# Newton's steps for the inverse roots of the norms, and the order of the first and last pair, in an attention and feed-forward kernel

## The chip, the cores and the metric

The kernel runs on one core of one Trainium2 chip. The core has five engines with a queue each: PE (TensorE, matrix products), DVE (VectorE), ACT (ScalarE), POOL (GpSimd) and SP (SyncE, which here issues transfers). Each engine works through its queue in order, and engines wait for each other through semaphores. The metric is the device time of one execution in microseconds.

## The reference

Eight batches of twelve heads, 448 positions, 64 values a head. Queries and keys are normalised by their root mean square and scaled with gains, then comes a softmax attention. Its output, seen as 3584 tokens of 768 values, goes through a feed-forward layer with a squared ReLU.

```python
def rmsnorm(x, g):
    rms = np.sqrt(np.mean(x * x, axis=-1, keepdims=True) + 1e-06)
    return x / rms * g
q_n, k_n = (rmsnorm(q, g_q), rmsnorm(k, g_k))
scores = scale * np.matmul(q_n, k_n.transpose(0, 1, 3, 2))
attn = np.exp(scores - max) / sum
x = (attn @ v).transpose(0, 2, 1, 3).reshape(B * S, H * D)
g = np.maximum(x @ w_in, 0.0) ** 2
out = g @ w_out
```

`w_in` and `w_out` come as 64-bit floats and are turned into 32-bit floats in the kernel.

## The kernel before, in words

The work is done by pairs of heads, so that 2 x 64 = 128 rows fill the array. There are 48 pairs. The feed-forward layer is a Strassen-Winograd product over two batches at a time (a span): seven products of half-size blocks in place of eight. Its weights' sums and differences are made once and kept in memory outside the core (`w1s`, `w2s`), from where blocks are streamed (`sw`).

The order of every instruction is written out by hand: inside the schedule the engines' queues hold the instructions in program order. Python generators interleave the strands of work.

**First stage.** `attention_alone` works on the first NAT = 12 pairs (two batches) with no product beside them. For pair i it does:

- `norm(i + 2)`: squares on ACT, sums over 64 values on DVE, the mean and 1e-6 on DVE, the inverse root on POOL as a power of -0.5 (L702, one value for each row, head and query or key: 112 x 16), and the queries times their factors on POOL (L704). The keys stay raw; their factors go into the exponentials as scales.
- `transpose(i + 1, s, n)`: four PE transposes into a bank of PSUM, and a copy to `qkT` on ACT. s = 1 are the keys, which wait only for their load; s = 0 the queries, which wait for L704.
- `scores(i, c)` for four chunks c of 112 keys: two matmuls (PE) and two exponentials (ACT).
- `values(i, ...)`: exponentials times values, on PE.
- `add_up(i, c)`: DVE adds the chunks' exponentials together in `acc` (L769). `total_of(i)` multiplies by ones on PE and so sums over keys: once for `acc`, which holds chunks 0 to 2, once for chunk 3.
- `finish(i)`: DVE turns the sums, takes their reciprocals and multiplies the outputs by them. `combine_x(i)` makes the differences that the first product needs (DVE, L849 to L854).

Pairs overlap: while pair i's scores are made, pair i-1's second half of values and its totals are. The function yields four times a pair. At each yield the caller takes a few steps of `weights`: the generator `prepare` makes one 128-row slice of the weights in four steps, with ACT (L580, L596), DVE (L593, L598, L603) and POOL. On POOL it adds halves (L568) and makes sums and differences (L574); each of these instructions has 128 x 384 elements. 52 such steps (EARLY) belong in the first stage, four of them before the first pair's scores and four more with its first yield. The other 88 lie beside the first product.

The norms of pairs 0 and 1 are made by another function, `normalise_in_turn` (L335), with powers of 112 x 8; pair 0's stands ahead of all else, in `first_pair`.

**Later stages.** `first_product` (L989) and `second_product` (L1036) alternate, with the attention of the next span woven into the second product. There the norms are `norm_by_squares`: DVE sums, a power on POOL of 128 x 28 (L724) and two products (L726).

The order in POOL's queue in the first stage is, pair by pair: L702, L704, then the weights' L568 and L574 of the four yields. So a late weights instruction makes the next pair's norm late, and PE's transposes of the queries with it.

Of the kernel before, what the change touches and what calls it, by code (L numbers as in the profile page):

```python
# [9 lines left out]
F32 = mybir.dt.float32  # L10
U32 = mybir.dt.uint32
AF = mybir.ActivationFunctionType
ALU = mybir.AluOpType
AX = mybir.AxisListType.X
# [372 lines left out]
def attention_then_ffn_bounded(  # L387
# [291 lines left out]
    def load_v(i):  # L679
# [5 lines left out]
        else:  # L685
            for h in range(2):
                nc.sync.dma_start(vs[i][:, h], v[b, h0 + h].rearrange("(j p) d -> p j d", j=NJ))

    def norm(i):
        if i >= NAT:  # L690
            squares(i)
            return norm_by_squares(i)
        raw, sq = (places_of(qk, i, n)[:SP] for n in range(2))
        rstd = rstds[i] = small.tile([SP, 2, 2 * NJ], F32, tag="rstd", name="rstd", bufs=4)
        normed[i] = sq[:, 0], raw[:, 1]
        if i == 1:
            return normalise_in_turn(nc, raw, sq, rstd, mhalf)
        nc.scalar.activation(sq, raw, AF.Square)
        nc.vector.tensor_reduce(rstd, sq.rearrange("p s (n d) -> p s n d", d=D), AX, ALU.add)
        nc.vector.tensor_scalar(rstd, rstd, 1.0 / D, 1e-6, ALU.mult, ALU.add)  # L700
        flat = rstd.rearrange("p s n -> p (s n)")
        nc.gpsimd.tensor_tensor(flat, flat, mhalf[:SP, 0:4 * NJ], ALU.pow)  # L702

        nc.gpsimd.tensor_tensor(sq[:, 0].rearrange("p (j h d) -> p h j d", j=NJ, h=2),  # L704
                                raw[:, 0].rearrange("p (h j d) -> p h j d", j=NJ, h=2),
                                rstd[:, 0].rearrange("p (h j) -> p h j ()", h=2).to_broadcast([SP, 2, NJ, D]),
                                ALU.mult)
# [5 lines left out]
    def norm_by_squares(i):  # L713
        raw, qkn = (by_squares(i, n) for n in range(2))
        NG = S // 32
        half = small.tile([P, 2 * NG], F32, tag="half", name="half")
        other = small.tile([P, 2 * NG], F32, tag="other", name="other")
        nc.vector.tensor_reduce(half, qkn.rearrange("p s g e -> p (s g) e"), AX, ALU.add)
        for n in range(4):
            m = n ^ 1  # L720
            nc.vector.tensor_copy(other[n * 32:(n + 1) * 32], half[m * 32:(m + 1) * 32])
        nc.vector.tensor_tensor(half, half, other, ALU.add)
        nc.vector.tensor_scalar(half, half, 1.0 / D, 1e-6, ALU.mult, ALU.add)  # L723
        nc.gpsimd.tensor_tensor(half, half, mhalf, ALU.pow)  # L724
        for s in range(2):
            nc.gpsimd.tensor_tensor(  # L726
                qkn[:, s], raw[:, s],
                half[:, s * NG:(s + 1) * NG].rearrange("p g -> p g ()").to_broadcast([P, NG, 32]), ALU.mult)
        normed[i] = qkn

    def transposes(i):
# [16 lines left out]
    def scores(i, c):  # L748

        at = i % 2 if i < NAT else 0  # L750
        sc = ps_s.tile([SP, 2, 512], F32, tag="s", name="sc")
        for h in range(2):
            rows = slice(h * D, (h + 1) * D)
            nc.tensor.matmul(sc[:, h, 0:S], qkT[rows, at, 1, c * SP:(c + 1) * SP], qkT[rows, at, 0, :],  # L754
                             start=True, stop=True)
        pr = probs[i, c] = places[(NJ * i + c) % len(places)][:SP]
        if i < NAT:
            for h in range(2):
                nc.scalar.activation(pr[:, h], sc[:, h, 0:S], AF.Exp, scale=rstds[i][:, 1, 2 * c + h:2 * c + h + 1])  # L759
        else:  # L760
            nc.scalar.activation(pr, sc[:, :, 0:S], AF.Exp)  # L761

    def acc_of(i):
        return sums[i % 2] if i < NAT else sums["acc"]

    def add_up(i, c):

        acc = acc_of(i)[:SP]
        nc.vector.tensor_tensor(acc, probs[i, 0] if c == 1 else acc, probs[i, c], ALU.add)  # L769
# [43 lines left out]
    def total_of(i):  # L813


        tots[i] = ps_o.tile([P, S], F32, tag="t", name="tot")
        for n, pr in enumerate((acc_of(i)[:SP], probs[i, NJ - 1])):
            for h in range(2):
                nc.tensor.matmul(tots[i][h * D:(h + 1) * D, :], sums["ones"], pr[:, h, :],  # L819
                                 start=(n == 0), stop=(n == 1))  # L820

    def finish(i):

        b, hp = divmod(i, NPAIR)
        pav, factors = pavs.pop(i), xT[:, b % 2, hp]
        x = factors
        if i < NAT:


            turned, factors = sums["turned"], sums["factors"]  # L830
            few = small.tile([P, S // 32], F32, tag="few", name="few")
            nc.vector.transpose(turned, tots.pop(i))
            nc.vector.reciprocal(few, turned.rearrange("p (g r) -> p g r", r=32)[:, :, 0])
            nc.vector.transpose(factors.rearrange("p (g r) -> p g r", r=32),
                                few.rearrange("p g -> p g ()").to_broadcast([P, S // 32, 32]))

            x = x.rearrange("d (p j) -> d j p", j=NJ)
            pav, factors = (t.rearrange("d (j p) -> d j p", j=NJ) for t in (pav, factors))
        nc.vector.tensor_tensor(x, pav, factors, ALU.mult)
        del vs[i]  # L840
# [15 lines left out]
    def attention_alone():  # L856


        for i in range(NAT):
            more = i + 1 < NAT  # L860
            if i + 3 < NAT:
                load(i + 3)
            scores(i, 0)
            scores(i, 1)
            if i + 2 < NAT:
                norm(i + 2)
            elif not more:
                norm(NAT)
                load(NAT + 2)
            add_up(i, 1)  # L870
            yield
            if i:
                transpose(i + 1, 1, 0) if more else None
                values(i - 1, (2, 3))
                total_of(i - 1)
                transpose(i + 1, 0, 0) if more else None
                finish(i - 1)
            load_v(i + 1)
            yield
            scores(i, 2)  # L880
            scores(i, 3)
            if i == 0:
                transpose(1, 0, 0)
                transpose(1, 1, 1)
            values(i, (0, 1))
            yield
            add_up(i, 2)
            if i:
                combine_x(i - 1)
            if NAT <= i + 3 < NAT + 2:  # L890
                load(i + 3)
            yield
        values(i, (2, 3))
        total_of(i)
        finish(i)
        combine_x(i)
# [181 lines left out]
    with tc.tile_pool(name="words", bufs=2) as spare["pool"]:  # L1078
        for _ in range(2):
            load_w(loaded[0])  # L1080
            loaded[0] += 1
        load(2)
        norm(1)
        with tc.tile_pool(name="first", bufs=2, reuse_waits="tile") as work:

            free = [gT[:, f] for f in range(NFC) if f % HF < HF - 2]
            places[:] = [g.rearrange("p (h q) -> p h q", h=2) for g in free[:2 * NJ]]
            sums[0], sums[1] = (g.rearrange("p (h q) -> p h q", h=2) for g in free[2 * NJ:2 * NJ + 2])
            sums["turned"], sums["factors"] = (g[:, 0:S] for g in free[2 * NJ + 2:2 * NJ + 4])
            sums["ones"] = work.tile([SP, D], F32, tag="ones", name="ones", bufs=1)  # L1090
            nc.vector.memset(sums["ones"], 1.0)
            weights(4)
            for u, _ in enumerate(attention_alone()):


                weights(min(EARLY, 8 + (EARLY - 8) * (u + 1) // (4 * NAT - 4)))
                if u == 4 * NAT - 6:
                    load_blocks(5)
        with tc.tile_pool(name="first_product", bufs=2, reuse_waits="tile") as work:
            for u, _ in enumerate(first_product(work, 0)):  # L1100
                if u == 6:

                    left = ps_s.tile([P, 2, 512], F32, tag="s", name="bits")
                    banks["bits"] = left.rearrange("p a b -> p (a b)")[:, 0:NW].bitcast(U32)
                weights(min(ALL, EARLY + (ALL - EARLY) * (u - 1) // (N1 - 6)))
                if u == N1 - 5:
                    norm(NAT + 1)
                if u == N1 - 4:
                    transposes(NAT)
                    squares(NAT + 2)  # L1110
# [24 lines left out]
def kernel(  # L1135
# [27 lines left out]
    def square_of_bound():  # L1163
# [5 lines left out]
        bound.tile([128, 8, 8 * D], F32, name="qk"),  # L1169
        bound.tile([128, 2, 2, S], F32, name="qkT"),  # L1170
        bound.tile([128, 128], F32, name="ident"),
        bound.tile([128, 2 * (S // 32)], F32, name="mhalf"),
        bound.tile([128, 2], F32, name="gains"),
        bound.tile([S // 4, 2, 8], F32, name="rstd0"),
        (load_gains, square_of_bound),
# [45 lines left out]
```

## Time and profile before

| what | before |
|---|---|
| time, median of 3 | 1406.08 us (1405.57 to 1407.02) |
| profiled span | 1404.7 us |
| PE busy | 98% of the span |
| DVE, ACT, POOL busy | 58%, 30%, 42% |
| L702, power of 112 x 16 | 10 times, 3583 ns each |
| L724, power of 128 x 28 | 36 times, 4827 ns each |
| L335, power of 112 x 8 | 4 times, 1709 ns each |
| L574 and L568 on POOL, first and second weights | 64 and 64 times, 1145 and 1147 to 1288 ns each |
| first stage ends (first matmul of the first product) | 139.9 us |

The shares of busy time are means over the whole span. Which engine a stage waits for is read from that stage's own window and from the chain of waits. POOL's power takes much longer than its size suggests, as each element costs it some 0.17 to 0.2 us.

### The profile page before, as it was taken

How to read it: one execution, taken by the hardware profiler on the slowest of the kernel's cores; microseconds unless marked ns; L12 is line 12 of the kernel's file. 1: busy time of each engine (PE TensorE's matmuls, PEld its weight loads, DVE VectorE, ACT ScalarE, POOL GpSimd, SP SyncE). 2: the span in 40 equal slices, each digit the busy share in tenths (PEclk: the TensorE clock that was granted, in tenths of full speed). 3: DMA queues.
4: the chain of work that ended last, by engine and by line, in shares of the span. 5: the costliest groups of instructions: out<-in, count | busy, mean ns of one | idle time of the engine just before them, and what ended most of it. 6: DMA issues, size and time to landing. Idle time of an engine off the chain costs nothing.

```text
span 1404.7 us, 14407 instructions
## 1 busy us (share of the span) xinstructions
PE 1377.9 (98%) x4422; PEld 636.9 (45%) x4422; DVE 813.5 (58%) x1402; ACT 420.3 (30%) x620; POOL 591.0 (42%) x400
## 2 busy tenths in 40 slices
PE   7998999999999999999999999999999999999998
PEld 3333445444444455544444455444444445554554
DVE  6999677489876333576777523457777633332111
ACT  7775565433332011233332011232333201110000
POOL 7999687544453022554344112445435302221000
PEclk9999999999999999999999999999999999999999
DMA  8767899645655433345576333345565333333443
GB/s 242 215 192 199 278 378 327 184 106 119 128 115 119 102 85 90 100 109 123 108 138 121 98 94 90 98 104 112 119 128 105 96 98 90 86 90 101 106 110 72
DMA packets 430914, 188.78 MB, mean 134 GB/s; under 512 B 277484, under 2 KB 428780, under 8 KB 430828
## 3 DMA queue, kind: packets, MB, share of 16 engines
q1 hardware_dynamic: 421228, 179.05, 49.2%
q10 hardware_dynamic: 9472, 8.72, 2.4%
q8 instruction: 37, 0.61, 0.2%
q14 instruction: 49, 0.40, 0.1%
q0 software_dynamic: 128, 0.00, 0.0%
HBM read 154.54 MB, written 33.16 MB: 134 GB/s over the span
## 4 chain that ended last, share of the span: by engine, by line
PE 91%; POOL 4%; DVE 2%; DMA 1%; issue 1%; ACT 1%; SPq 0%; POOLq 0%; DVEq 0%
PE ps L1036 37%; PE pa L989 10%; PE pd L989 10%; PE pc L989 10%; PE sc L754 9%; PE pav L810 9%; PE pb L989 5%; POOL rstd L702 1%; POOL gC L568 1%; DMA sw<-w1s 1%; DVE gT L769 0%; DMA gT<-in_moe_w_in_dram 0%; POOL qk L704 0%; PE tot L819 0%; POOL gC L574 0%
## 5 line engine op out<-in xcount | busy, mean ns | idle before, releaser
L1036 PE MATMUL ps<-gT,sw 128*128 128x448 f32 x768 | 299.2, 542 | 0.8 <-POOL gT L966 0.8
L724 POOL TENSOR_TENSOR half<-half,mhalf 128x28 f32<-128x28 f32 x36 | 173.8, 4827 | 259.7 <-DVE half L723 227.7
L1036 PE MATMUL ps<-gC,sw 128*128 128x448 f32 x576 | 225.2, 542 | 0.0
L966 POOL TENSOR_TENSOR gT<-gT 128x448 f32<-128x448 f32 x96 | 93.5, 976 | 311.9 <-ACT gT L962 311.9
L1036 PEld LDWEIGHTS ps<-gT,sw 128*128 128x128 f32 x768 | 143.9, 190 | 151.0 <-issue 147.5
L761 ACT ACTIVATE pr<-sc 112x896 f32<-112x896 f32 x120 | 104.8, 915 | 296.4 <-PE sc L754 205.6
L754 PE MATMUL sc<-qkT 64*112 64x448 f32 x768 | 171.8, 567 | 6.1 <-ACT gT L759 3.9
L1036 PEld LDWEIGHTS ps<-gC,sw 128*128 128x128 f32 x576 | 108.0, 190 | 112.3 <-issue 111.4
L989 PE MATMUL pa<-xT,sw 128*128 128x448 f32 x384 | 156.2, 543 | 0.4 <-DMA sw<-w1s 0.4
L962 ACT ACTIVATE gT<-gT 128x448 f32<-128x448 f32 x96 | 55.3, 576 | 309.6 <-DVE gT L1004 309.6
L754 PEld LDWEIGHTS sc<-qkT 64*112 64x112 f32 x768 | 61.6, 173 | 104.7 <-issue 80.5
L989 PEld LDWEIGHTS pa<-xT,sw 128*128 128x128 f32 x384 | 73.4, 192 | 73.8 <-issue 73.3
L810 PE MATMUL pav<-pr,vt 112*64 112x448 f32 x480 | 100.2, 547 | 0.0
L726 POOL TENSOR_TENSOR qk<-qk,half 128x448 f32<-128x448 f32 x72 | 84.9, 1198 | 2.8
L769 DVE TENSOR_TENSOR acc<-acc,pr 112x896 f32<-112x896 f32 x60 | 68.1, 1135 | 19.1 <-ACT pr L761 16.2
L1004 DVE TENSOR_TENSOR gT<-z,pd 128x448 f32<-128x448 f32 x32 | 19.8, 620 | 101.2 <-PE pd L989 101.2
L989 PE MATMUL pd<-xT,sw 128*128 128x448 f32 x192 | 77.9, 542 | 0.0
L989 PE MATMUL pb<-xC,sw 128*128 128x448 f32 x192 | 77.4, 539 | 0.0
L989 PE MATMUL pc<-xC,sw 128*128 128x448 f32 x192 | 77.4, 539 | 0.0
L989 PE MATMUL pd<-xC,sw 128*128 128x448 f32 x192 | 77.4, 539 | 0.0
L989 PE MATMUL pc<-xT,sw 128*128 128x448 f32 x192 | 77.4, 539 | 0.0
L574 POOL TENSOR_TENSOR gC<-gC 128x384 f32<-128x384 f32 x64 | 72.2, 1145 | 2.5
(120 smaller groups left out, 1564.2 us busy)
## 6 DMA issues: line engine op xcount, KB each, us to landing
sw<-w1s SPq DMA_DIRECT2D x224, 192.0 KB, 2.3
sw<-w2s SPq DMA_DIRECT2D x168, 256.0 KB, 3.2
w1s<-gC SPq DMA_DIRECT2D x8, 1344.0 KB, 7.5
w2s<-gC SPq DMA_DIRECT2D x8, 1344.0 KB, 8.4
out_dram<-osb SPq DMA_DIRECT2D x184, 56.0 KB, 1.9
qk<-in_q_dram SPq DMA_DIRECT2D x144, 56.0 KB, 2.9
qk<-in_k_dram SPq DMA_DIRECT2D x144, 56.0 KB, 2.7
vt<-in_v_dram SPq DMA_DIRECT2D x72, 112.0 KB, 2.8
```

The lines of the kernel that those rows point to most:

```text
L574: nc.gpsimd.tensor_tensor(*[blocks_of(n)[:, i] for i in (dst, x, y)], op)
L724: nc.gpsimd.tensor_tensor(half, half, mhalf, ALU.pow)
L726: nc.gpsimd.tensor_tensor(qkn[:, s], raw[:, s], half[:, s * NG:(s + 1) * NG].rearrange("p g -> p g ()").to_broadcast([P, NG, 32]), ALU.mult)
L754: nc.tensor.matmul(sc[:, h, 0:S], qkT[rows, at, 1, c * SP:(c + 1) * SP], qkT[rows, at, 0, :], start=True, stop=True)
L761: nc.scalar.activation(pr, sc[:, :, 0:S], AF.Exp)
L769: nc.vector.tensor_tensor(acc, probs[i, 0] if c == 1 else acc, probs[i, c], ALU.add)
L810: nc.tensor.matmul(pavs[i][h * D:(h + 1) * D, :], vs[i][:, h, c, :], probs[i, c][:, h, :], start=(c == 0), stop=(c == NJ - 1))
L962: nc.scalar.activation(g, src, AF.Relu)
L966: nc.gpsimd.tensor_tensor(g, g, g, ALU.mult)
L989: nc.tensor.matmul(ps, stream[n + i][:, c], rhs[:, c], start=first and c == 0, stop=c == HC - 1, skip_group_check=not first)
L1004: add(g, x, ps, ALU.add)
L1036: nc.tensor.matmul(ps, stream[n][:, c % 4], rhs_of[i][:, c], start=c == 0, stop=c == HF - 1)
```

## The change

Three things are done.

1. The inverse root is no longer POOL's power but an estimate from the number's bits, followed by three of Newton's steps: one instruction and three times four, all on POOL, on 112 x 16 or 128 x 28 values. Half the mean square is kept in `half`, the root in `rstd` (or `other`), the step's intermediate in `step`. The powers of 112 x 8 for the first two pairs stay. It is to make POOL's part of a norm shorter.
2. Pair 0 gets an order of its own: all four chunks of scores and exponentials, both transposes of pair 1, two additions and the norm of pair 2 come ahead of the first weights' step. It yields once in place of four times. For the pairs behind it, the values and totals of the pair before move ahead of `norm(i + 2)`, and the rate of the weights' steps is fitted to the new number of yields.
3. For pair 11 (`i + 1 == NAT`) the addition of chunk 2 is left out, and `total_of` multiplies chunk 2 by ones on PE instead: three parts in place of two.

```diff
+    def inverse_roots(y, half):
+        t = small.tile(list(y.shape), F32, tag="step", name="step", bufs=1)
+        nc.gpsimd.tensor_scalar(y.bitcast(U32), half.bitcast(U32), -0.5, float(0x5EF759DF), ALU.mult, ALU.add)
+        for _ in range(3):
+            nc.gpsimd.tensor_tensor(t, y, half, ALU.mult)
+            nc.gpsimd.tensor_tensor(t, t, y, ALU.mult)
+            nc.gpsimd.tensor_scalar(t, t, -1.0, 1.5, ALU.mult, ALU.add)
+            nc.gpsimd.tensor_tensor(y, y, t, ALU.mult)
...
-        nc.vector.tensor_reduce(rstd, sq.rearrange("p s (n d) -> p s n d", d=D), AX, ALU.add)
-        nc.vector.tensor_scalar(rstd, rstd, 1.0 / D, 1e-6, ALU.mult, ALU.add)
-        flat = rstd.rearrange("p s n -> p (s n)")
-        nc.gpsimd.tensor_tensor(flat, flat, mhalf[:SP, 0:4 * NJ], ALU.pow)
+        half = small.tile([P, 2 * (S // 32)], F32, tag="half", name="half")[:SP, 0:4 * NJ]
+        half = half.rearrange("p (s n) -> p s n", s=2)
+        nc.vector.tensor_reduce(half, sq.rearrange("p s (n d) -> p s n d", d=D), AX, ALU.add)
+        nc.vector.tensor_scalar(half, half, 0.5 / D, 0.5e-6, ALU.mult, ALU.add)
+        inverse_roots(*[t.rearrange("p s n -> p (s n)") for t in (rstd, half)])
...
-        nc.vector.tensor_scalar(half, half, 1.0 / D, 1e-6, ALU.mult, ALU.add)
-        nc.gpsimd.tensor_tensor(half, half, mhalf, ALU.pow)
+        nc.vector.tensor_scalar(half, half, 0.5 / D, 0.5e-6, ALU.mult, ALU.add)
+        inverse_roots(other, half)
...
-        for n, pr in enumerate((acc_of(i)[:SP], probs[i, NJ - 1])):
+        parts = [acc_of(i)[:SP]] + [probs[i, c] for c in range(2 if i + 1 == NAT else 3, NJ)]
+        for n, pr in enumerate(parts):
...
-            few = small.tile([P, S // 32], F32, tag="few", name="few")
+            few = small.tile([P, S // 32], F32, tag="few", name="few", bufs=1)
...
             scores(i, 0)
             scores(i, 1)
+            if i == 0:
+                transpose(1, 1, 1)
+                scores(0, 2)
+                scores(0, 3)
+                transpose(1, 0, 0)
+                add_up(0, 1)
+                add_up(0, 2)
+                norm(2)
+                load_v(1)
+                values(0, (0, 1))
+                yield
+                continue
+            if more:
+                transpose(i + 1, 1, 0)
+            values(i - 1, (2, 3))
+            total_of(i - 1)
             if i + 2 < NAT:
                 norm(i + 2)
...
             add_up(i, 1)
             yield
-            if i:
-                transpose(i + 1, 1, 0) if more else None
-                values(i - 1, (2, 3))
-                total_of(i - 1)
-                transpose(i + 1, 0, 0) if more else None
-                finish(i - 1)
+            if more:
+                transpose(i + 1, 0, 0)
+            finish(i - 1)
             load_v(i + 1)
             yield
             scores(i, 2)
             scores(i, 3)
-            if i == 0:
-                transpose(1, 0, 0)
-                transpose(1, 1, 1)
             values(i, (0, 1))
             yield
-            add_up(i, 2)
-            if i:
-                combine_x(i - 1)
+            if more:
+                add_up(i, 2)
+            combine_x(i - 1)
...
-            weights(4)
             for u, _ in enumerate(attention_alone()):
-                weights(min(EARLY, 8 + (EARLY - 8) * (u + 1) // (4 * NAT - 4)))
-                if u == 4 * NAT - 6:
+                weights(min(EARLY, 4 + (EARLY - 4) * u // (4 * NAT - 7)))
+                if u == 4 * NAT - 9:
                     load_blocks(5)
```

The tile `mhalf`, which holds the exponent -0.5, shrinks from 28 to 8 columns, since only the powers of 112 x 8 use it.

## The prediction, made before the changed kernel was run

> **What bounds the kernel now.** I read the page, then the busy time by stage, the chain of waits, and single engines' timelines through the first stage.
>
> ```profile
> PE 1377.9 (98%) x4422; PEld 636.9 (45%) x4422; DVE 813.5 (58%) x1402; ACT 420.3 (30%) x620; POOL 591.0 (42%) x400
> ...
> 53.10:96.50 43.40, 40.07 (x208) 15.34 (x208) 39.81 (x48) 33.94 (x57) 42.77 (x26) 1.00 0.70 214
> 160.00:240.00 80.00, 79.56 (x212) 39.84 (x211) 58.89 (x72) 50.99 (x79) 64.16 (x62) 1.00 1.00 367
> 268.00:1404.00 1136.00, 1129.23 (x3506) 526.79 (x3504) 609.71 (x1130) 249.36 (x347) 371.88 (x233) 1.00 0.45 105
> ```
>
> The last three lines give window, length, busy time of PE, PEld, DVE, ACT, POOL, granted clock, DMA share, GB/s. From 160 us on PE hardly stops, so what is won before moves the end one to one. Only the first stage (12 pairs alone, to 140 us) has room, and there POOL is full: 42.77 of 43.40 us. The chain of waits of that stretch:
>
> ```profile
> 57.64 2.15 issue
> 59.78 1.01 POOL gC L574
> 60.79 2.28 POOL gC L568 x2
> 63.07 3.59 POOL rstd L702
> 66.66 0.07 issue
> 66.73 1.04 POOL qk L704
> 67.77 3.38 POOL gC L568 x2
> ```
>
> The power (L702) and the queries' product (L704) stand in one queue with the weights' work (L568, L574). PE's timeline shows the four places that matter:
>
> ```profile
> 16.00 3.23 PE L754 MATMUL sc<-qkT 64*112 64x448 f32 x8 [3.90 <-ACT gT L759]
> ...
> 23.42 1.76 PE L754 MATMUL sc<-qkT 64*112 64x448 f32 x8 [1.44 <-ACT qkT L744]
> ...
> 120.05 0.60 PE L742 MATMUL pt<-ident,qk 112*128 112x112 f32 x4 [1.43 <-POOL qk L704]
> ...
> 136.70 3.26 PE L819 MATMUL tot<-gT,ones 112*64 112x448 f32 x8 [3.00 <-DVE gT L769]
> ...
> 143.50 2.42 PE L989 MATMUL pb<-xC,sw 128*128 128x448 f32 x6
> ```
>
> The exponentials of pair 0 come late (3.90); PE waits for POOL before each pair's query transposes (the last at 120.05); it waits for the last addition (3.00) and then runs slow, 3.26 us where the same totals otherwise take 1.67. From pb (143.50) it is fed.
>
> **What the Trainium skill says.** GPSIMD Engine Reference, 2.1 Instruction dispatch: a Pool instruction that reads what another core wrote must wait for the producer's completion; here each Newton step carries such a wait, and the trace shows its price, 0.07 us from L702 to L704. SBUF — State Buffer, Who interferes with whom: a VectorE instruction with two SBUF inputs, or in a 2-port mode, and a GpSimd one that reads SBUF lock each other out whole. The trace agrees: two L574 in a row take 3.36 us beside an addition and a clamp, 1.97 alone. TensorE: Matmul & The Clock Gate, Part 1: an idle window of about 3.4 us halves the clock. The trace agrees in kind, with less: the slow matmuls at 16.00 and 136.70 come after idles of 3.90 and 3.00, while 1.43 at 120.05 left the clock alone.
>
> **The change part by part.**
>
> *Newton in place of power.* Ten powers of 112x16, shortest 3.22 us (33.72 to 119), become 13 small instructions each, every one waiting for the one before. No row shows a small two-input POOL instruction. Bounds: from below a MEMSET of one element per partition, 0.10, plus the 0.07 wait, 0.17 each, 2.2 us in all. From above: L574 (384 elements, 0.99) and L849 (448, 1.13) give 2.25 ns an element and 0.125 us fixed, so 0.16 for 16 elements; 0.17 to 0.18 with spread, plus 0.07, 0.24 each, 3.1 us. I take 2.2, as four of the 13 have one input. The 36 powers of 128x28 (4.8 us) go the same way, but lie in stages where PE waits for POOL 0.8 us in all: nothing.
>
> *What the power hid.* While it runs it keeps no DVE instruction out, nor is it kept out: at 43.30 it took 3.22 with the combine L603 (0.96) and the addition L769 (1.08) inside. Thirteen instructions that each read SBUF can be stopped between any two by such a DVE instruction. From the end of L704 at 38.06 to the one at 120.00 are 8 pairs at 10.24 us. POOL's own: 3.22 + 1.04 + four weights instructions at 1.00 + waits 0.15 = 8.41; the excess 1.83 is lock. DVE's lockable work per pair: two additions 2.16, L593 0.50, L598 0.56, L603 0.96, in all 4.18; 2.04 of it inside the power, so 2.14 cost 1.83: 0.86 of it is paid.
>
> *New pitch.* The instruction order has 34 weights instructions in the same 8 pairs (4.25 each pair) and DVE work of 39.3 us (17 additions, 10 L593, 10 L598, 9.5 L603, 2 subtractions), 4.9 a pair, none hidden by a power. If 0.86 were paid it would be 4.2 a pair. I take 0.70, 3.4: POOL starts with some 3 us in hand so the first pairs don't pay, and 13 waits of 0.07 are open to DVE. Pitch: 2.2 + 1.11 + 4.25 + 0.08 + 3.44 = 11.08, so 88.6 us for 8 pairs, longer than before, with a start that is earlier.
>
> *First pair.* Its key factors are there at 10.05 (8.41 + 1.64). Scores run 9.02 to 12.1; exponentials of two chunks end at 13.3 (4 x 0.55 behind the second chunk), the key copy at 13.9, the other two chunks 16.25, the query copy 16.9, so PE reaches pair 1's scores at 17 and not 23.42. Squares of pair 2 end at 18, as before (16.87 + 1.07), so norm(2) on POOL starts at 19.5 as before. Then ACT has three passes of 0.91 for the weights (20.7), exponentials (22.9), copy and squares (24.5), DVE 1.4 (25.9): norm(3) ends at 25.9 + 2.2 + 0.07 + 1.04 = 29.3. Before, it ended at 38.06, but six weights instructions stood ahead of it, now none. So the last query product ends at 29.3 + 88.6 = 117.9, against 120.0.
>
> *Tail.* From pair 11's query transposes: 0.55, scores and values 1.69 + 1.65 + 1.69 + 1.65 (7.2), total of pair 10 1.5, scores 1.69, values 3.3, total of pair 11 in three parts 2.3: 16. Then on DVE transpose 0.64, reciprocal 0.24, transpose 0.65, product 1.0, subtraction 0.61. DVE's queue ahead of these (square sums 2.2, addition 1.08, finish 2.5, subtractions 1.9) ends about there too; pb starts some 20.5 after the transposes, before 143.50 - 120.05 = 23.45. The addition taken out (1.08), the 3.00 wait and the slow clock pay for the 0.8 of extra matmul. 117.9 + 20.5 = 138.4: pb 5.1 us earlier. The smaller buffers (few, step) are used by one engine in order: nothing.
>
> *After pb* the weights' steps per block are unchanged and the streams keep the DMA at 1.00 with PE waiting 0.44 us in 80: no gain or loss taken. 1406.1 - 5.1 = 1401.0.
>
> **The rivals.**
> PE-bound: if POOL falls out of the chain, PE's own pitch holds, 9.27 (totals at 27.19 and 36.45). Norm(2) ends at 19.5 + 2.2 + 1.1 = 22.8; from there transposes, scores, values, scores, transposes, values (0.55 + 1.69 + 1.65 + 1.69 + 0.53 + 1.65) bring pair 1's total to 30.6 and pair 10's, nine pitches on, to 114.0. Pair 11's transposes stand 7.2 before it, at 106.8, and pb 20.5 to 21 behind them, 127.8: 15.7 earlier, 1390.4. For it: PE's pitch of 9.27 to 9.35 up to 46 us. Against: POOL would need 9.27 in all, and 2.2 + 1.1 + 4.3 leave 1.6 for 4.9 of lockable DVE work.
>
> Slower: Newton costs 3.1 and 0.86 of DVE's work is paid. Pitch 3.1 + 1.11 + 4.25 + 0.08 + 4.2 = 12.75, 102 us; norm(3) ends at 30.1, the last product at 132.1, pb at 152.6: 9.1 later, 1415. With 0.70 paid, or with 2.2 and 0.86, it is 1409 and 1407. For it: the lock is plain in the trace, and PE would idle 3 us a pair, enough for a slow clock. Against: those ends of both costs must come together.
>
> No change: start and tail gains eaten by the longer pitch, as with Newton at 2.6 and 0.75 paid (pitch 11.72, last product 123.5, pb 144.0, 1406.6); the band is 1403.3 to 1408.9.
>
> **How the numbers follow.** Forecast (1396 to 1403.3) 0.40; PE-bound or near it 0.16; within 0.2% 0.14; slower 0.30. Faster is the first two, 0.56. I put the forecast first because both unknown costs have a middle that is near its values, and start and tail are read off rows. The range, 1389.5 to 1413.5, takes in the PE-bound time and most of the slower cases, and leaves out the far end of Newton's cost with full lock and cold clock.
>
> **What would show it.** In the profile after: pair 1's first scores near 17 us; the span of one Newton group start to start (2.2 to 3.1 alone, longer beside additions); the query product of pair 11 ending at 117.9; no wait for an addition ahead of the last totals, and full speed there; pb at 138.4. If POOL is out of the chain of waits by 60 us, the PE-bound rival holds. If L568 and Newton's steps fill POOL at over 12 us a pair, the slower one does. If PE waits for streamed weights in the first product by more than 0.5 us, my last step was wrong.

## The result, and the profile after

The changed kernel takes 1425.76 us (median; 1425.41 to 1427.47) where the kernel before takes 1405.9 (one run more than in the table above). The ratio is 1.0142, with an interval of 1.0125 to 1.016. I had forecast 1401.0 and a range up to 1413.5, so it went the other way, and beyond my range. The first stage holds the loss. First the line of the page after, then the busy time by stage (window, length, busy time of PE, PEld, DVE, ACT, POOL, granted clock, DMA share, GB/s):

```profile
PE 1384.1 (97%) x4426; PEld 639.8 (45%) x4426; DVE 805.9 (57%) x1401; ACT 421.7 (30%) x620; POOL 578.5 (41%) x952
```

```profile
24.60:139.00 114.40, 91.76 (x432) 35.22 (x432) 81.65 (x112) 73.69 (x119) 101.52 (x162) 0.90 0.63 172
290.00:1423.00 1133.00, 1125.82 (x3494) 525.46 (x3492) 611.56 (x1129) 247.19 (x343) 346.85 (x637) 1.00 0.45 105
```

POOL is busy for less time in all (578.5 against 591.0 us), and yet its part of the first stage is longer. PE stands still for 22.6 of the 114.4 us between pair 2's query transposes and pair 11's; the granted clock there is 0.90. In the last stages PE works 99% of the time, as before. PE's timeline shows where it stands:

```profile
19.28 1.67 PE L832 MATMUL tot<-gT,ones 112*64 112x448 f32 x8
24.69 0.89 PE L754 MATMUL pt<-ident,qk 112*128 112x112 f32 x4 [3.73 <-POOL qk L716]
25.51 3.11 PE L766 MATMUL sc<-qkT 64*112 64x448 f32 x8
...
59.19 1.01 PE L754 MATMUL pt<-ident,qk 112*128 112x112 f32 x4 [5.02 <-POOL qk L716]
...
83.56 1.01 PE L754 MATMUL pt<-ident,qk 112*128 112x112 f32 x4 [2.68 <-POOL qk L716]
...
113.77 1.01 PE L754 MATMUL pt<-ident,qk 112*128 112x112 f32 x4 [6.99 <-POOL qk L716]
...
139.01 1.01 PE L754 MATMUL pt<-ident,qk 112*128 112x112 f32 x4 [5.12 <-POOL qk L716]
...
160.91 2.49 PE L1013 MATMUL pb<-xC,sw 128*128 128x448 f32 x6 [1.04 <-issue]
```

The start is early as meant: pair 0's totals begin at 19.28 (before: 27.19). Then PE waits for the query product, now L716, five times, 23.5 us in all (before 6.9 us in eight waits). Each of these waits, from 2.68 us up, is followed by slow matmuls (3.11 us for scores that take 1.76); two waits of 1.36 and 1.15 us for additions are not (the totals behind them take 1.72). Pair 11's query transposes come at 139.01 where they came at 120.05, pb at 160.91 where it was 143.50. Those 17.4 us are nearly all of the 18.9 between the two profiled spans. The other 1.5 lie behind pb, where PE now waits once for a block of streamed weights:

```profile
171.30 2.49 PE L1013 MATMUL pd<-xC,sw 128*128 128x448 f32 x6 [1.14 <-DMA sw<-w1s]
```

What POOL does in between, from the end of pair 3's query product (32.54) to that of pair 11 (138.95), by groups (line, engine, operation, names and shapes, count, busy us and mean ns, idle before):

```profile
L574 POOL TENSOR_TENSOR gC<-gC 128x384 f32<-128x384 f32 x16 | 20.5, 1294 | 0.6
L695 POOL TENSOR_TENSOR step<-rstd,half 112x16 f32<-112x16 f32 x24 | 12.1, 504 | 1.9
L697 POOL TENSOR_SCALAR step<-step 112x16 f32<-112x16 f32 x24 | 9.9, 414 | 2.1
...
L696 POOL TENSOR_TENSOR step<-step,rstd 112x16 f32<-112x16 f32 x24 | 7.4, 307 | 1.9
L693 POOL TENSOR_SCALAR rstd<-half 112x16 uint32<-112x16 uint32 x8 | 6.6, 829 | 2.5 <-DVE half L713 1.9
L698 POOL TENSOR_TENSOR rstd<-rstd,step 112x16 f32<-112x16 f32 x24 | 6.2, 258 | 2.0
```

In this stretch POOL stands idle for more than 0.3 us only once (1.95 us at 34.5, for DVE's sums of squares). So it sets the pace, and what the slow clock costs PE does not lengthen this stretch directly.

Newton's instructions are busy for 42.2 us, and with the waits between them a group takes 6.3 us from its first instruction to the product, over the eight norms. The power took 3.66 to the same point in the kernel before. Two things make the 6.3, and both stand in POOL's timeline of one norm:

```profile
53.91 0.22 POOL L695 TENSOR_TENSOR step<-rstd,half 112x16 f32<-112x16 f32 x1
54.21 0.22 POOL L696 TENSOR_TENSOR step<-step,rstd 112x16 f32<-112x16 f32 x1
54.52 0.20 POOL L697 TENSOR_SCALAR step<-step 112x16 f32<-112x16 f32 x1
54.81 0.22 POOL L698 TENSOR_TENSOR rstd<-rstd,step 112x16 f32<-112x16 f32 x1
55.11 2.01 POOL L695 TENSOR_TENSOR step<-rstd,half 112x16 f32<-112x16 f32 x1
57.20 0.22 POOL L696 TENSOR_TENSOR step<-step,rstd 112x16 f32<-112x16 f32 x1
```

and in DVE's timeline of the same moment:

```profile
55.08 1.08 DVE L781 TENSOR_TENSOR gT<-gT 112x896 f32<-112x896 f32 x1
56.09 0.95 DVE L603 SCALAR_TENSOR_TENSOR gC<-words,gC 128x768 uint32<-128x768 uint32 x1
```

Undisturbed, the instructions start 0.30 us apart: 0.20 to 0.22 of their own and 0.08 of wait. Thirteen of them are 3.9 us (one group, at 90.79, has nothing in its way and takes 3.88), so the chain alone is longer than the power it replaces (3.22 at its shortest in the kernel before, 2.90 where nothing holds it up, as the first experiment shows). And the step at 55.11 takes 2.01 us: an addition of DVE and, right behind it, a combine of the weights keep it out. This is the lock of the prediction.

### The profile page after: what moved, and what is told of

The parts are those of the page before. It is cut to its first block, busy times and chain, and to the rows that moved or that the text cites. A ratio compares the mean times of both kernels' runs of the same rounds, so it can differ in the third digit from the quotient of the medians.

```text
span 1423.6 us, 14961 instructions
## 1 busy us (share of the span) xinstructions
PE 1384.1 (97%) x4426; PEld 639.8 (45%) x4426; DVE 805.9 (57%) x1401; ACT 421.7 (30%) x620; POOL 578.5 (41%) x952
## 4 chain that ended last, share of the span: by engine, by line
PE 90%; POOL 4%; DMA 3%; ACT 1%; issue 1%; DVE 1%; SPq 0%; ACTq 0%; POOLq 0%
PE ps L1060 36%; PE pd L1013 10%; PE pa L1013 10%; PE pc L1013 10%; PE sc L766 10%; PE pav L822 9%; PE pb L1013 5%; DMA sw<-w1s 1%; DMA qk<-in_k_dram 1%; POOL gC L568 1%; DMA qk<-in_q_dram 1%; POOL step L695 1%; POOL gC L574 1%; POOL step L697 1%; POOL step L696 0%
## 5 line engine op out<-in xcount | busy, mean ns | idle before, releaser
L766 PE MATMUL sc<-qkT 64*112 64x448 f32 x768 | 176.0, 578 | 0.9 <-ACT qkT L383 0.8
L693 POOL TENSOR_SCALAR other<-half 128x28 uint32<-128x28 uint32 x36 | 9.7, 268 | 251.8 <-DVE half L735 251.8
L781 DVE TENSOR_TENSOR acc<-acc,pr 112x896 f32<-112x896 f32 x60 | 71.1, 1185 | 17.9 <-ACT pr L773 15.4
L738 POOL TENSOR_TENSOR qk<-qk,other 128x448 f32<-128x448 f32 x72 | 77.4, 1096 | 2.8
```

Of the source, the lines that this page charges most:

```text
L738: nc.gpsimd.tensor_tensor(qkn[:, s], raw[:, s], other[:, s * NG:(s + 1) * NG].rearrange("p g -> p g ()").to_broadcast([P, NG, 32]), ALU.mult)
```

## The experiments

Each was timed beside the kernel before, and its ratio is to that. Theory A: Newton's 13 instructions on POOL make the loss in the first stage, by their length and by the lock. Theory B: the new order of pair 0 and of the weights makes it. Theory C: Newton in the later stages costs. All kernels but the last pair's total alone and one addition on the kernel before keep the smaller buffer `few` as well.

**The power back in the first stage only.**

```diff
 # norm(i), first stage; the rest is the changed kernel
...
-        inverse_roots(*[t.rearrange("p s n -> p (s n)") for t in (rstd, half)])
...
+        nc.vector.tensor_scalar(rstd, rstd, 1.0 / D, 1e-6, ALU.mult, ALU.add)
...
+        nc.gpsimd.tensor_tensor(flat, flat, mhalf[:SP, 0:4 * NJ], ALU.pow)
```

> The changed kernel with the power put back in the norms of the first stage only (L716's factors come from one power again); first pair's order, last pair's total and Newton in the later stages stay. Theory A (Newton's 13 instructions on POOL, 0.30 us each and each open to the lock, make the loss in the first stage): the loss goes and the gains of the first and last pair remain, 1396 to 1404 us. Theory B (the new order of the first pair and of the weights' steps makes the loss, Newton about as long as the power): still 1418 or more. Theory C (Newton in the later stages costs): still well above before, 1410 to 1420.

Measured: 1406.41 us, ratio 1.0012 (1.0003 to 1.0021). The loss is gone, so Newton in the first stage made it, and B and C fall. But in the median nothing of the first and last pair's gains remains, which A had put at 2 to 9 us. PE's waits in its profile (us in all, times, longest):

```profile
PE pt L753 <- POOL qk L715: 5.6, 4, 2.4
PE pav L821 <- DMA vt<-in_v_dram: 2.0, 1, 2.0
...
PE tot L831 <- DVE gT L780: 1.6, 2, 1.4
PE pb L1012 <- issue: 1.1, 1, 1.1
```

The waits for POOL are nearly as in the kernel before (5.6 us against 6.9). Pair 1's total begins at 32.53 (before 36.45), pair 10's at 126.83 (before 127.18): the early start is lost again pair by pair. POOL needs 10.85 us a pair from pair 3's query product (31.20) to pair 11's (118.00), before 10.24; the product itself, L715, takes 1.61 us on average where L704 took 1.11. The profile is that of the fastest of the 20 runs, 2.4 us under the median. In it pb comes at 139.11, 4.4 us earlier than before, and 1.9 of these are lost behind pb, where PE waits 1.9 us for streamed weights (before 0.4).

This profile also corrects my reading of the power. On POOL and on DVE, at three places:

```profile
35.02 4.35 POOL L713 TENSOR_TENSOR rstd<-rstd,mhalf 112x16 f32<-112x16 f32 x1 [1.02 <-DVE rstd L711]
34.85 1.08 DVE L780 TENSOR_TENSOR gT<-gT 112x896 f32<-112x896 f32 x1
35.86 0.56 DVE L593 TENSOR_SCALAR gC<-gC 128x768 f32<-128x768 f32 x1
...
47.90 2.93 POOL L713 TENSOR_TENSOR rstd<-rstd,mhalf 112x16 f32<-112x16 f32 x1
48.36 0.97 DVE L603 SCALAR_TENSOR_TENSOR gC<-words,gC 128x768 uint32<-128x768 uint32 x1
49.23 1.09 DVE L780 TENSOR_TENSOR gT<-gT 112x896 f32<-112x896 f32 x1
...
57.85 2.90 POOL L713 TENSOR_TENSOR rstd<-rstd,mhalf 112x16 f32<-112x16 f32 x1
```

Once under way, the power meets a combine and an addition at no cost to either side (47.90). But at its start it is kept out like any other POOL instruction: at 35.02 by an addition and a clamp, for some 1.4 us. The 3.22 us that I took for undisturbed in the kernel before had such a wait in it: the power at 43.30 began while DVE's L598 ran until 43.75.

**Newton alone, on the kernel before.**

```diff
 # the kernel before, norm(i)
...
-        nc.gpsimd.tensor_tensor(flat, flat, mhalf[:SP, 0:4 * NJ], ALU.pow)
...
+        inverse_roots(*[t.rearrange("p s n -> p (s n)") for t in (rstd, half)])
 # norm_by_squares
...
-        nc.gpsimd.tensor_tensor(half, half, mhalf, ALU.pow)
+        inverse_roots(other, half)
```

> The kernel before with Newton's steps in place of both powers and nothing else. Theory A: slower than the changed kernel or equal to it, 1422 to 1435 us, since the gains of first and last pair are missing. Theory B: about as before, 1404 to 1409.

Measured: 1427.85 us, ratio 1.0164 (1.0146 to 1.0182). A holds: Newton alone gives the whole loss. A group takes 5.8 us here on average.

**Two of Newton's steps in place of three.**

```diff
-        for _ in range(3):
+        for _ in range(2):
```

> The changed kernel with two of Newton's steps in place of three (the roots are then good to some 5e-6): 9 instructions instead of 13. Theory A, chain and lock: 4 x 0.30 = 1.2 us less a norm and with it a third of the lock paid in Newton's group (some 0.5), for 8 to 10 norms 10 to 17 us: 1409 to 1416. If only the lock counted and not the number of instructions: 1422 or more.

Measured: 1414.61 us, ratio 1.0065 (1.0045 to 1.0085), 11.2 us less than the changed kernel, as A had it. The mean group falls from 6.26 (all ten norms) to 4.39 us: 1.2 are the four instructions, 0.67 are lock. This run also parts length from lock. Where nothing meets them, nine instructions need less than the power's 2.90 and its wait:

```profile
113.09 0.20 POOL L693 TENSOR_SCALAR rstd<-half 112x16 uint32<-112x16 uint32 x1
...
115.76 1.04 POOL L716 TENSOR_TENSOR qk<-qk,rstd 112x512 f32<-112x512 f32 x1
```

That is 2.67 us to the product, and yet the kernel is 8.2 us slower than the one with the power in the same place and order (1406.41). So the lock alone is enough for a loss.

**No additions of chunks on DVE.**

```diff
-        parts = [acc_of(i)[:SP]] + [probs[i, c] for c in range(2 if i + 1 == NAT else 3, NJ)]
+        parts = [probs[i, c] for c in range(NJ)]
 # and every add_up(...) of the first stage left out
```

> The changed kernel with no additions of chunks on DVE in the first stage: all four chunks go through the ones on PE. It takes 2.2 us a pair of two-input DVE work away and adds 1.5 us a pair of matmul. If the lock beside the additions costs POOL nearly their length (theory A), POOL's pitch falls by some 2 us a pair from 13.3 and the stage by 15 us, to about 1408 to 1413, and Newton's group is seen near 3.9 us where no other DVE instruction meets it. If the lock is not what lengthens it, the extra matmuls show: 1426 or more.

Measured: 1408.0 us, ratio 1.0021 (1.0014 to 1.0029), 17.8 us less than the changed kernel, although PE has 1.5 us more to do for a pair. Here PE is full in the first stage (again window, length, busy PE, PEld, DVE, ACT, POOL):

```profile
25.00:124.00 99.00, 98.71 (x506) 38.20 (x507) 59.76 (x90) 72.76 (x119) 83.62 (x162) 0.98 0.70 197
```

Newton's group falls to 5.24 us on average. So the additions do hold POOL up; the other 1.3 us over 3.9 are mostly the weights' DVE instructions, which are still there (at 51.09 a step of 0.22 takes 0.97 beside the combine). The forecast that the group would be seen near 3.9 holds only where none of these meets it.

**The power in all norms.** As the first experiment, and in `norm_by_squares` too.

> The changed kernel with the power back in all norms, first and later stages; order of the first pair and total of the last stay. If Newton in the later stages lies beside other work, the same as with the power in the first stage alone: 1404 to 1409 us. If it cost time there (36 norms), 1400 or less.

Measured: 1405.44 us, ratio 1.0007 (0.9998 to 1.0016), against 1.0012 with Newton in the later stages. Those 36 norms lie beside other work, whichever way they are made.

**The last pair's total alone, on the kernel before.**

```diff
-            add_up(i, 2)
+            if more:
+                add_up(i, 2)
 # total_of: three parts for the last pair
```

> The kernel before with the last pair's chunk 2 summed on PE and not added on DVE, nothing else. My step for the tail gave 3 us for this and the shorter queue of DVE together. The wait of 3.00 us before the last totals and the slow clock after it go: 1402 to 1405 us. If DVE's queue only moves the wait to the subtractions ahead of the second block: no change, 1405 to 1407.

Measured: 1403.24 us, ratio 0.9988 (0.9981 to 0.9995): 1.7 us won (0.7 to 2.7 by the interval). From pair 11's query transposes to pb it took 20.1 us (120.50 to 140.57) in place of 23.45. In the two profiles pb is 2.9 us earlier and the span 3.2 shorter, but the profile of before is of a run somewhat slower than the median beside this experiment (1406.5 against 1404.8), so the ratio is the better measure.

**The order of the first pair alone**, with the power everywhere and the last pair's addition back (`range(3, NJ)` and an `add_up(i, 2)` for every pair).

> The changed kernel with the power everywhere and the last pair's addition back: only the order of the first pair and the rate of the weights are left. If POOL's queue sets the pace of all pairs behind the first, PE's early start is eaten and the stage ends as before: 1405 to 1410 us. If the early start were kept: 1400 to 1402.

Measured: 1406.38 us, ratio 1.0009 (1.0003 to 1.0016). The order wins nothing, and by the interval costs 0.4 to 2.2 us. In the profile, of its fastest run, pair 3's query product ends at 30.32 (before 38.07) and pair 11's at 117.42 (before 120.00): POOL's queue takes most of the early start back.

**One addition a pair, with the power.** A version that should beat both.

```diff
 # the changed kernel with the power everywhere
-        parts = [acc_of(i)[:SP]] + [probs[i, c] for c in range(2 if i + 1 == NAT else 3, NJ)]
+        parts = [acc_of(i)[:SP]] + [probs[i, c] for c in range(2, NJ)]
-            if more:
-                add_up(i, 2)
 # and pair 0's add_up(0, 2)
```

> A version meant to beat both: power everywhere, and chunk 2 of every pair summed on PE in three parts, so DVE adds once a pair. It takes 1.1 us a pair of lockable DVE work off POOL's queue and puts 0.8 us a pair on PE (pitch 9.27 to 10.0). If POOL at over 10 us a pair is still the limit, PE's extra lies in its waits: 1398 to 1404 us. If PE becomes the limit at once: 1404 to 1410.

Measured: 1401.54 us, ratio 0.9978 (0.9971 to 0.9985): faster than both. In its profile the totals come every 10.01 us through most of the stage, which is PE's own pitch, with one longer gap of 15.5. Beside the same order and power with two additions (1.0007) the step is clear.

**The same on the kernel before.**

> The kernel before with chunk 2 of every pair summed on PE and one addition a pair on DVE, nothing else. If the gain of the version with power and one addition comes from the lockable DVE work taken out, and not from the order of the first pair: the same, 1400 to 1403 us. If it needs the new order: 1403 to 1406.

Measured: 1402.64 us, ratio 0.9984 (0.9976 to 0.9991). The interval overlaps that of the version with the new order. But it overlaps that of the last pair's total alone just as well (0.9981 to 0.9995), and pb comes at 139.94, only 0.6 us ahead of that run's. So in the old order it isn't shown that the other pairs' additions win anything; in the new order the step from 1.0007 to 0.9978 shows it.

**Fewer steps of the weights in the first stage**, with both additions and with one.

```diff
-    EARLY, ALL = 4 * 13, 4 * (2 * NFC + 3)
+    EARLY, ALL = 4 * 11, 4 * (2 * NFC + 3)
```

> Order of the changed kernel, power everywhere, both additions, and 44 steps of the weights in the first stage in place of 52 (the other 96 beside the first product). If POOL's queue is the first stage's limit, 8 steps less, 8 instructions of 1.0 us and the lock beside them, take up to 8 us off the stage: 1397 to 1402 us. If the first product cannot take more of them (the DMA is full there), its waits for streamed weights give it back: 1403 or more.

> Both: one addition a pair, power everywhere, new order, and 44 steps of the weights in the first stage. With one addition PE's own pitch (10.0) is the limit of most pairs, so fewer steps can only take away the last waits for POOL (3.7 us): 1398 to 1402 us. If the first product pays for the moved steps: 1402 to 1406.

Measured: 1401.05 us, ratio 0.997 (0.9961 to 0.9979) with both additions, and 1401.75 us, 0.9971 (0.9963 to 0.998) with one. Work taken out of POOL's queue wins about 4 us, at the lower end of what was hoped. In the first of the two, pb is at 131.43 in its profile, 12.1 us earlier than before, while that profile's span is only 8.1 us shorter: the first product waits for streamed weights (1.1, 0.5 and 0.3 us) and for DVE (0.9), and gives a third of it back. (The run of that profile is 2.7 us under its median.) The two remedies don't add up, although they do in the first stage: with both, pb comes at 132.83, 5.6 us before one addition alone (138.41), but from pb to the end it takes 1267.3 us against 1263.5 there and 1261.2 before. PE waits for DVE (2.5 and 0.8 us) in the first product, which has the moved steps beside it.

## Why the prediction was wrong, point by point

- **What bounds the kernel now: right.** POOL bounds the first stage and PE all the rest; 17.4 of the 18.9 us are there at pb. Against my sum pb is 22.5 us late (160.91, forecast 138.4): 3.2 in norm(3), 17.8 in the eight pairs, 1.4 in the tail.
- **"I take 2.2, as four of the 13 have one input": the step that failed.** Newton's group costs 3.9 us undisturbed, above even my upper bound of 3.1. I worked the fixed part of a small POOL instruction out of large ones, 0.125 us; it is 0.19 (0.222 at 16 columns and 0.243 at 28 give 1.75 ns a column). The one-input instructions, which I thought cheap, take 0.205. And the lower bound, a MEMSET, reads nothing. Over the eight pairs the error is 8 x 1.68 = 13.4 us, the largest part of the 17.8, and two more norms ahead of them have it. The wait that each step carries, which I took from L702 and L704, was right (0.07, measured 0.08).
- **"Nor is it kept out": wrong.** DVE instructions that run when the power begins do keep it out. Undisturbed it takes 2.90 us and not 3.22. With 2.90, my sum for the kernel before has 8.09 of POOL's own and 2.15 of lock for 2.14 of DVE's work: by this estimate nearly all of it was paid, and not 0.86. So the trace gave even less ground for a share below that.
- **"I take 0.70": the second term too small.** In the changed kernel the lock cost Newton's groups 6.34 - 3.88 = 2.46 us a pair, and the weights' instructions 1.4 us (45.6 us for 35 of them that need 1.0 or a little less). That is 3.9 us a pair where I had 3.44; of DVE's 4.9 it is 0.79, above my 0.70. The pitch was 106.4 / 8 = 13.3 us; forecast 11.08.
- **First pair.** PE reached pair 1's scores at 15.5, earlier than the 17 forecast. Norm(3) ended at 32.54 and not at 29.3: its group began at 24.75, earlier than the 25.9 forecast, but took 6.75 us to the product in place of 2.27. The gain that I carried from there to the end does not exist by itself (ratio 1.0009 for the order alone).
- **Tail.** 21.9 us from 139.01 to pb, forecast 20.5, before 23.45. The direction was right, and there was no wait for an addition ahead of the last totals, which ran at full speed, as forecast. Alone it is worth 1.7 us. Here the slow matmuls after the 5.12 us wait took 2.5 us more for three groups (1.01, 3.33 and 2.25 in place of 0.60, 1.76 and 1.72).
- **After pb, "no gain or loss taken": wrong by 1.5 us.** My own sign for it came, a wait for streamed weights of 1.14 us in the first product.
- **Later stages at nothing: right** (1.0012 with Newton there, 1.0007 without).
- **The rival.** "Slower" named the mechanism, 3.1 and 0.86 giving 12.75 us a pair and 1415. I had its clearest sign in hand, 2.04 us a pair of DVE work hidden inside the power, and priced the loss of that hiding too low because I set both unknowns near their cheap ends. Even its 1415 lay outside my range. With 3.9 and 0.79, the sum of that rival is 3.9 + 1.11 + 4.25 + 0.08 + 3.9 = 13.2, nearly the pitch of 13.3.

PE's long waits come at every second pair and not at each. The traces show with what this goes: between two query products POOL takes 14.0 to 18.0 us where three of DVE's additions fall in between, and 10.4 to 12.2 where one does, and each of the last four long waits stands at the end of a stretch with three. Why the additions fall so unevenly stays open.

## What to carry to other kernels

Count the instructions before their elements: a chain of small dependent ones has a price for each link (here 0.30 us), and one long instruction may be cheaper although it looks wasteful for its size. Look at what else runs during the long instruction; if the replacement can be stopped where the long one ran on, its own length is only a part of its cost (here 1.0 of the 3.1 us by which a pair became longer). On a queue that sets the pace, take work out of the queue; here the earlier start in front of it was lost again. And look where the work goes that is taken out: the first product gave part of the gain back.

## What the runs showed of the hardware

- A small POOL instruction in a dependent chain costs 0.30 us: 0.222 (two inputs, 112 x 16), 0.243 (128 x 28) or 0.205 to 0.215 (one input), and 0.08 to the next one's start.
- POOL's power grows evenly with the columns: undisturbed 1.64 us for 8, 2.90 for 16 (first experiment), 4.80 for 28 (these on 128 partitions). An estimate from these three is 0.38 us and 0.158 a column. The 0.17 to 0.2 us of the table's reading hold the fixed part and the waits as well.
- The power is kept out by a DVE instruction only at its start (4.35 us at 35.02, beside an addition and a clamp). Later a combine and an addition run inside it at full speed (0.97 and 1.09), and it takes 2.93.
- An addition of DVE (L781) with another such instruction right behind it keeps a waiting POOL step out of both: 2.01 us for a step of 0.22 beside an addition (1.08) and a combine (0.95). So it was in all 11 cases of the changed kernel's first stage. Behind a combine a step did get in ahead of the next addition, in all four cases. On POOL and DVE:

```profile
40.91 0.92 POOL L696 TENSOR_TENSOR step<-step,rstd 112x16 f32<-112x16 f32 x1
40.79 0.96 DVE L603 SCALAR_TENSOR_TENSOR gC<-gT,gC 128x768 uint32<-128x768 uint32 x1
41.67 1.11 DVE L781 TENSOR_TENSOR gT<-gT 112x896 f32<-112x896 f32 x1
```

The step ends at 41.83, behind the combine (41.75) and long before the addition (42.77).
